# A gated mix of a state-space convolution and a linear attention on one core: the order of all steps, the engines of the evictions and the PSUM rings made anew

## The chip, the cores and the metric

The kernel runs on one core of one Trainium2 chip. The metric is the device time of one execution in microseconds (us); the times given are medians of several runs. A profile is taken of one execution. The core's engines are TensorE (PE; PEld is its weight load), VectorE (DVE), ScalarE (ACT), GpSimd (POOL) and SyncE (SP). SP only issues transfers and waits; the transfers themselves run on 16 DMA engines.

## The reference, cut to what matters

```python
# x, u: [1, 2048, 512] bf16
def _A_ref(u, ...):                       # a long convolution for each of 512 channels
    P = jnp.exp(logdA[:, :, None] * l)    # 512 channels x 128 states x 2048 steps
    K = jnp.einsum("dn,dnl,dn->dl", Cc, P, dB).real
    y = irfft(rfft(pad(u)) * rfft(pad(K)))[..., :L]
    return y + u * Dskip

def _B_ref(x, wqkv, w_phi, wo):           # 32 heads of 16
    q, k, v = split(x @ wqkv)
    phi_q = concat(softmax(q @ w_phi), softmax(-(q @ w_phi)))   # phi_k likewise
    kv = einsum("bhsf,bhsd->bhfd", phi_k, v);  z = phi_k.sum over s
    o = (phi_q @ kv) / (phi_q . z + 1e-6)
    return o @ wo

x = A_u
g = sigmoid((x * gate_w).sum(-1))
return g * _A_ref(x, ...) + (1 - g) * _B_ref(x, ...)
```

## The kernel before

The program is not written in the order in which it runs. Functions such as `prepare`, `attention_keys`, `plan_queries` and `plan_conv` add 1058 steps ("nodes") to a `Plan`, each with a name, an engine or a choice of two, the steps it depends on, and the buffers of named rings that it takes and gives back. `Plan.run` then calls the steps one after the other in the order that the string `ORDER` gives (two digits a step). Two more strings settle the choices: `SIDES` has a digit for each step that may run on either of two engines (nearly all of them copy a PSUM tile to SBUF: evictions), and `RINGS` has one for each PSUM tile that may come from either of two rings of two buffers, `ps`, and `p0` or `pf`. Each engine runs its own instructions strictly in the order in which they were recorded; what waits for another engine or a transfer holds all that stands behind it on that engine. For SP these are the issues of transfers: a transfer that waits for its data holds the transfers behind it.

```python
order = [64 * code[a] + code[b] for a, b in zip(self.ORDER[0::2], self.ORDER[1::2])]
...
n.at = n.eng if isinstance(n.eng, str) else n.eng[int(next(sides, 0))]
...
for i in order:
    n = self.nodes[i]
    ...
    n.fn()
```

In time the program has these stretches. (1) Loads, tables of sines, folding of w_phi into the weights (tiles wT, wps, WW, Wqp), transposes of x (xps to xT). (2) The keys of the attention in 16 blocks (pk, Ek, Zk, vp, vb, vr, kvp) with the first half of the Fourier transform of u beside them (psA to XAu, psB to xst, written to DRAM as XUd). (3) The second half of that transform with the polar tables of the convolution (Ctab, Dtab). (4) For 16 units of 32 channels: the kernel K of the convolution is made by a matmul of generated factors (cs, E, R, A to kps to KD), transformed (psA to XA, psB to XK), multiplied by u's transform, which is read back from DRAM (XUX; the product is t, lines L1231 and L1234), and transformed back (psz to Zr, written to DRAM as Zd and read back turned as ZT, then psy, then xT at L1367 or L1370); the queries of the attention run beside it (pq, Eq, apm, ax, ops, oT). (5) The last units, and the output's transfers (out_dram, L992 and L1384).

The channels are treated in four groups Q0 to Q3 of 128. Q0 to Q2 go through the transforms in one piece each; Q3 goes in three: 64 channels (units 12 and 13), 32 (unit 14) and 32 (unit 15, which skips the way over DRAM: tiles Z, L1373). In the profile the transfers of the first of these pieces are Zd_0_122, those of the second Zd_64_123. A product t needs a load XUX; there are three buffers for these loads. The string `FOURS` marks the units whose sum of two halves of A is left to TensorE (step A3, L1109, is then empty).

Of the kernel before, what the change touches and what calls it, by code (L numbers as in the profile page):

```python
# [70 lines left out]
class Plan:  # L71

    DIGITS = "0123456789abcdefghijklmnopqrstuvwxyzABCDEFGHIJKLMNOPQRSTUVWXYZ-_"
    ORDER = ("190H0I0405060B0C0D0d0e0f0y0z0A0s0t0u000K0L1d0J0M0S0U0V0N0_0P0Q2R11122x0O100W0T13142S0X0Y162T2U0708090g0h0i0j0k0l2y010203"
             "0m0n0o0a0b0c2V2X0Z15171a1H1b2v0R0-2Y2Z2W2L1c1n1o0p0q0r1w2M2-2_181y302J2K1e1f1p1z1A1I1J2w2B1x1E2D35312E1g1Y2C0v0w0x0E0F0G"
             "2F321N1B2G2H1C2I33361P372P1O2N341F382Q393b1q1r1s2O4C2z3c4J4K4L4M3d4Y4Z4-3a3e4N4O4_3f4Q3h3g1D4U3j4P1R4R4V4W4S5350573k4T3i"
             "511S544X52555b5c5d5e3l1G581Q3n595i5f5m3m5g3o1T5n5h5j565a3p3r3s5o1U3q3R5k3S5q5r5s5x1L4D5t3w4E3y5u3x3t3u3v5l5p5B5y5F1V5v5H"
             "3D1M5C3z2A5w5G3F5z5A5D3G4F5E5I5U5V5W3T3A3B3C3E5X5J5M5N5K5L5O4G5Q5Y5R5Z3K3M5S3U5_1Z635P5T3N5-1h1i1j1k1l1m6067691W643V6162"
             "65683H3I3J666m3W3L6o3O3P3Q3X3Z3-6a6n6p3Y6b6c1K6q3_6d6r6s414043421X441-27201_4546474828492129224a23246e2d2b252a4b4g4c2e2c"
             "2f2h1t1u1v266f2j2g4i4d4e4f2i4h4j4k4l4m4n2o2l2q2p6i2k2s4o4p4q4r4s4t2r6j4u4w4v4x2m2t2n6g6k6t4y4z4A6x6u2u8n6y6v4B8r6z8k8o8m"  # L80
             "8q6h6l6w6A6B8l6G8w4H8x8p8t4I6F8s8u6I6K8y6H8z6L8v8A8C9e9f9g8Q6M7d8D8I8E6N6J8R8B7f9b9c9d7g8F6O7h7j6P8S7i8G6Q8H8J8W8Z7Ma_b0"
             "b17k8K7e6R6S8T6C6D6E7O8-7Q6T8_8L7N7R8M8X6U6V6W937l8O8U8N8V7mae7S8P8Yaf7n7o94907p9192agan7Taoa4ap7q7P6X6Y6Z6_70716-7r7s7t"
             "a8a995a572ak73ah7u7v7w96aaa6ab9774at98aial7y7z7A7599a776aj9a7x77acau78am797aaqar9n9o7C9v7Uadasav9w7V9paw7B9xaKaLaBaC7D7W"
             "9q9raHaD9y7X7YaIaQaE9z9D9E7E7F7Zc5c6bXb_9L9Mc0aM7b9k9l9maFaxay9h9i9j9F7-7_80aGazaA7GbYc1aJ7HaR9A9B9C818283858687aNaOaP7I"
             "7cb-aYaZa-7JaSc784c3aT9Ncb88bZc8899s9t9uc29GaU9H9O8aaVc98b8dc49P9I9J9Kcc8fceaW8gcfaX7Kb5b6b78e8ccacdb8ckb97Lcgch8h8ibg8j"
             "cBclcibabhcCdYdZbocjcmbpcncDcHbicscvd-cIeLbb9Q9R9S9T9U9Vctcubjcyb2b3b4d_e0bq9W9X9YbccScTcU9Ze1e2eMbwbdbebfcwbke3co9-bxe4"
             "cPcQcRe5cqczblbmbncxe6e7e8cpbycreUdOeVcVcWcXcAcE9_cFcGa0eNa1dRcJe9eaebdSdTeRdWbrcKbscLcNeOePeSecbzcMcOc_bAdPdQedeeefeWd0"
             "dUeQbtbubvd1a2d7a3egd8bBbCbDeTdVcYcZc-d2e-d9dad3dfdneXbEbFbGdbe_bKeYbLdgdheZdodXfAf0d4d5d6dcdddefBdpbMdidqf1djehdrfCeibN"
             "fDf2bHbIbJf4g1f3eCeDeEdkdldmdsdtduf5bOf6fGg2fEf7fHfefFg7fIezeAeBfJffdBg4f8fgfKbPg3f9g5g8g6fLfadvdwdxbQfhdCdydzdAfbfcfddE"
             "fMdFfiejfNdGg9fjfkfldHekeFeGeHgaeleIeJeKgbepfmfnfoemgcfOfpfqfrfPeneofQbRbSbTeqerdDdIdJdKgdgegfgggifsghgjfRfSfTfUbUbVbWgk"  # L90
             "eseteuevfVfWfXfYfZf-glgmgngodLdMdNftfxfyfzgpfufvfwewexeygqgrf_g0gsgtgugvgwgx")
    SIDES = ("111110110010111010001100101000101000111000001011110000000000111110110001001110000010001000000000000000000000000000000000"
             "00000000000000000100000000000000000000000001011110101")
    RINGS = ("100100101110111011000000000000000000000000100000000000000000111101000000001010101111100111010001001100101011001111100110"
             "11000")
# [1535 lines left out]
```

## Time and profile before

| | |
|---|---|
| median of 3 runs | 263.15 us (263.0 to 264.77) |
| the profiled execution | 265.59 us, its span 263.8 us |
| busy, share of the span | DVE 88%, ACT 84%, PE 75%, PEld 51%, POOL 4% |
| mean granted TensorE clock | 0.92 |
| transfers | 36.19 MB, 137 GB/s in the mean |

The span runs from the first instruction to the last; 1.79 us of the execution lie around it. A share of busy time is a mean over the stretches above, which have different limits, so the prediction reads the busy time stretch by stretch. An engine's instructions overlap at their ends: two evictions of 128x1024 that take 1.02 us each stand in 1.94 us.

### The profile page before, as it was taken

What the parts mean: (1) busy time and instruction counts of PE and PEld (TensorE: products, weight loads), DVE (VectorE), ACT (ScalarE), POOL (GpSimd) and SP (SyncE); (2) the same over time, 40 slices, a digit from 0 to 9 for tenths busy, and PEclk for the clock granted to TensorE, in tenths of its full rate; (3) what the DMA queues carried; (4) which work ended last, traced back from release to release, by engine and by line L of the source; (5) the groups of instructions that cost most, each with busy time, mean ns of one, the idle gap of its engine ahead of it and who ended that gap; (6) DMA issues with size and microseconds to landing.
All of it is one profiled execution on the core that took longest, in us unless ns stands there. A gap on an engine that the chain in (4) does not pass through costs nothing.

```text
span 263.8 us, 10077 instructions
## 1 busy us (share of the span) xinstructions
PE 199.0 (75%) x4492; PEld 135.1 (51%) x4512; DVE 231.0 (88%) x314; ACT 221.2 (84%) x305; POOL 11.4 (4%) x22
## 2 busy tenths in 40 slices
PE   0576799999948569888498666799977698898650
PEld 0475566755735333445357354475864376774540
DVE  6799799898799998999999998999999989974440
ACT  7968998888899999999999999999999887665000
POOL 4650000000000000000000000000000000000000
PEclk9999999999995797999858988999999799999875
DMA  7799000362731676505250567366957788859875
GB/s 192 134 193 221 2 4 0 112 161 46 218 72 41 183 220 192 169 6 151 53 162 5 159 158 185 75 166 166 226 153 182 179 177 206 190 191 158 195 92 93
DMA packets 67259, 36.19 MB, mean 137 GB/s; under 512 B 46352, under 2 KB 62864, under 8 KB 66832
## 3 DMA queue, kind: packets, MB, share of 16 engines
q1 hardware_dynamic: 66160, 35.42, 55.2%
q8 instruction: 35, 0.57, 0.9%
q10 hardware_dynamic: 1056, 0.13, 0.3%
q14 instruction: 8, 0.07, 0.1%
HBM read 22.17 MB, written 13.37 MB: 135 GB/s over the span
## 4 chain that ended last, share of the span: by engine, by line
ACT 31%; PE 30%; DVE 22%; issue 7%; DMA 6%; POOL 1%; SPq 1%; ACTq 0%; DVEq 0%; POOLq 0%
ACT cs L68 6%; PE pk L705 5%; DMA XUX<-XUd 5%; PE vp L753 4%; ACT E L68 3%; PE psz L1263 3%; ACT Eq L68 3%; ACT XK L145 3%; ACT XA L145 2%; ACT Zr L145 2%; ACT xst L145 2%; PE kvp L770 2%; ACT L65 2%; PE psA L587 2%; PE psA L186 2%
## 5 line engine op out<-in xcount | busy, mean ns | idle before, releaser
L1098 DVE TENSOR_TENSOR A<-Ctab,Dtab 128x2048 bf16<-128x2048 bf16 x32 | 38.8, 1221 | 1.5 <-PE kps L179 1.5
L68 ACT ACTIVATE cs<-args 128x1024 bf16<-128x1024 f32 x32 | 30.8, 1060 | 0.5 <-PE args L1020 0.5
L179 PE MATMUL kps<-R,A 128*32 128x64 bf16 x1536 | 18.3, 205 | 6.9 <-issue 2.0
L179 PEld LDWEIGHTS <-A 128*32 128x32 bf16 x1536 | 16.2, 118 | 11.6 <-issue 5.9
L1116 DVE TENSOR_TENSOR R<-E,cs 128x2048 bf16<-128x2048 bf16 x16 | 19.5, 1221 | 0.6 <-ACT E L68 0.5
L1120 DVE TENSOR_TENSOR R<-E,cs 128x2048 bf16<-128x2048 bf16 x16 | 19.5, 1221 | 0.0
L68 ACT ACTIVATE Ek<-pk 128x512 bf16<-128x512 f32 x32 | 16.7, 603 | 2.5 <-PE pk L705 2.5
L1231 DVE TENSOR_TENSOR t<-XUX,XK 128x2048 bf16<-128x2048 bf16 x14 | 17.0, 1222 | 1.5 <-ACT XK L145 1.5
L145 ACT CAST XA<-psA 128x1024 bf16<-128x1024 f32 x15 | 15.2, 1040 | 3.3 <-PE psA L186 3.3
L145 ACT CAST Zr<-psz 128x1024 bf16<-128x1024 f32 x15 | 15.5, 1035 | 2.9 <-ACT cs L68 0.9
L1263 PE MATMUL psz<-t,TI 128*128 128x512 bf16 x53 | 16.0, 412 | 2.2 <-DVE xT L1370 0.6
L753 PE MATMUL vp<-WW,xT 128*128 128x512 bf16 x58 | 16.3, 406 | 1.0 <-issue 0.8
L68 ACT ACTIVATE E<-args 128x1024 bf16<-128x1024 f32 x16 | 16.8, 1059 | 0.2 <-PE args L1042 0.2
L839 PE MATMUL pq<-xT,Wqp 128*128 128x512 bf16 x64 | 16.5, 395 | 0.6 <-ACT Eq L68 0.6
L68 ACT ACTIVATE Eq<-pq 128x512 bf16<-128x512 f32 (+1 forms) x28 | 16.6, 698 | 0.1
L145 ACT CAST XK<-psB 128x1024 bf16<-128x1024 f32 x15 | 15.3, 1024 | 1.6 <-PE psB L192 1.5
L612 PE MATMUL psB<-XAu,TB 64*128 64x128 bf16 x256 | 11.3, 248 | 5.8 <-ACT xst L145 3.9
L705 PE MATMUL pk<-WW,xT 128*128 128x512 bf16 x58 | 14.7, 380 | 0.4 <-issue 0.2
L186 PE MATMUL psA<-W,KD 128*64 128x128 bf16 x256 | 11.2, 237 | 4.7 <-ACT cs L68 2.7
L612 PEld LDWEIGHTS <-TB 64*128 64x128 bf16 x256 | 9.4, 109 | 9.0 <-issue 8.9
L192 PE MATMUL psB<-XA,TB 128*128 128x128 bf16 (+2 forms) x192 | 10.2, 201 | 4.9 <-DVE XA L147 1.6
L186 PEld LDWEIGHTS <-KD 128*64 128x64 bf16 x256 | 9.2, 119 | 8.1 <-issue 5.7
(210 smaller groups left out, 503.5 us busy)
## 6 DMA issues: line engine op xcount, KB each, us to landing
XUX<-XUd SPq DMA_DIRECT2D x32, 256.0 KB, 4.1
XUd<-xst SPq DMA_DIRECT2D x8, 512.0 KB, 3.0
ax<-apd SPq DMA_DIRECT2D x16, 256.0 KB, 4.1
Zd<-Zr SPq DMA_DIRECT2D x15, 256.0 KB, 3.0
ZT<-Zd SPq DMA_DIRECT2D x12, 256.0 KB, 5.4
UD<-in_A_u_dram SPq DMA_DIRECT2D x16, 128.0 KB, 4.3
XUd<-xst SPq DMA_DIRECT2D x8, 256.0 KB, 3.8
wqk<-in_B_wqkv_dram SPq DMA_DIRECT2D x1, 1024.0 KB, 6.5
```

The lines of the kernel that those rows point to most:

```text
L68: return self.nc.scalar.activation(**kw)
L145: self.nc.scalar.copy(out=o, in_=i)
L179: nc.tensor.matmul(kps[32 * dj:32 * dj + 32, g4, e, :], lhsT=A[:, d // 4, 32 * ka:32 * ka + 32, d % 4], rhs=R[:, kr, d, :], start=(i == 0) ...
L186: nc.tensor.matmul(ps[64 * ri:64 * ri + 64], lhsT=lhsT, rhs=fc.W1[:, ri].rearrange("p r d -> p (r d)"), start=True, stop=True, tile_positi ...
L612: nc.tensor.matmul(box.ps[:, c2, sl, :], lhsT=fc.TB[rows, b0:b0 + 2].rearrange("p a b -> p (a b)"), rhs=X.t[rows, k, r0 + sl].rearrange("p ...
L705: nc.tensor.matmul(box.ps[:], lhsT=xT[:, st, kt, :], rhs=g.WW[:, kt, :], start=(kt == 0), stop=(kt == 3))
L753: nc.tensor.matmul(box.ps[:], lhsT=xT[:, st, kt, :], rhs=g.WW[:, 4 + kt, :], start=(kt == 0), stop=(kt == 3))
L1098: nc.vector.tensor_tensor(out=c.A[:, :, 64 * k:64 * k + 64, :].rearrange("p q (x b) l -> p x b q l", b=8), in0=cf.unsqueeze(2).to_broadcas ...
L1116: nc.vector.tensor_tensor(out=c.R[:, :, :, 32:64], in0=t.E[:, 1].unsqueeze(1).to_broadcast([128, 2, 32, 32]), in1=t.cs[:], op=ALU.mult)
L1120: nc.vector.tensor_tensor(out=c.R[:, :, :, 0:32], in0=t.E[:, 0].unsqueeze(1).to_broadcast([128, 2, 32, 32]), in1=t.cs[:, ::-1, :, ::-1], o ...
L1231: nc.vector.tensor_tensor(out=box.t, in0=Ls[r0 // ns].X[:], in1=box.XK[:].unsqueeze(1).to_broadcast([128, 2, 1024]), op=ALU.mult)
L1263: nc.tensor.matmul(box.ps[:, hb, :], lhsT=fc.TIp[:, k].rearrange("p h a t -> p (h a t)"), rhs=box.t[:, k, 512 * hb:512 * hb + 512], start= ...
```

## The change

`ORDER`, `SIDES` and `RINGS` are replaced. No step is added or removed, the rings have as many buffers as before, and `FOURS`, which marks eight units, reads the same.

```diff
 class Plan:
-    ORDER = ("190H0I0405060B0C0D0d0e0f0y0z0A0s0t0u000K0L1d0J0M0S0U0V0N0_0P0Q2R11122x0O100W0T13142S...
+    ORDER = ("0405060B0C0D0H0d0e0f0y0z0A190s0t0u0708090I0J0M000L11120g0h0i0j0k0l0K0102030_2R0S0T10...
...
-    SIDES = ("111110110010111010001100101000101000111000001011110000000000111110110001001110000010001...
+    SIDES = ("101110000101100010001000101110100001101100001011100000000000000000100010010100101001000...
...
-    RINGS = ("100100101110111011000000000000000000000000100000000000000000111101000000001010101111100...
+    RINGS = ("000111101111001111000000000000000000000000100000000000000010001110100000101010101101010...
...
     FOURS = ("0111100101011000")
```

Of the steps with a choice of engine, 24 go from DVE to ACT (8 vb, 3 xT of the transposes, 3 oT, 2 XK, 2 xst, and one each of XAu, KD, wT, wps, Z and the Ctab copy of psy), 17 from ACT to DVE (4 of L978, 3 oT, 2 XAu, 2 xst, 2 vb, 2 xT of the transposes, one UDp, one xT of bps), and one from POOL to DVE (Wphi, L469). Three places of the order follow.

SP, the last stretch. The rows are transfers: XUX is a load of u's transform for unit 12 and up, Zd and ZT the way of a piece over DRAM and back, out_dram the output. Before:

```order
L1289 DMA ZT<-Zd_0_121 32x4096 x4
L1279 DMA Zd_0_122<-Zr 128x1024 x2
L1185 DMA XUX<-XUd 128x1024 x4
L1289 DMA ZT<-Zd_0_122 32x32x64 x4
L1384 DMA out_dram<-xT 32x12x256 x2
L1384 DMA out_dram<-xT 32x12x128 x2
L1279 DMA Zd_64_123<-Zr 128x1024
L1384 DMA out_dram<-xT 32x12x256 x2
L992 DMA out_dram<-xT 32x4x384 x2
L1289 DMA ZT<-Zd_64_123 32x32x32 x4
L1384 DMA out_dram<-xT 32x12x128 x2
L1384 DMA out_dram<-xT 512x1x64 x4
```

Four more stand behind these rows: two of L992 and two of 512x1x64. The same stretch after the change:

```order
L1185 DMA XUX<-XUd 128x1024 x2
L1289 DMA ZT<-Zd_0_121 32x4096 x4
L1279 DMA Zd_0_122<-Zr 128x1024 x2
L1185 DMA XUX<-XUd 128x1024 x2
L1289 DMA ZT<-Zd_0_122 32x32x64 x4
L1384 DMA out_dram<-xT 32x12x128 x4
L1279 DMA Zd_64_123<-Zr 128x1024
L1384 DMA out_dram<-xT 32x12x256 x4
L1289 DMA ZT<-Zd_64_123 32x32x32 x4
L1384 DMA out_dram<-xT 512x1x64 x2
L992 DMA out_dram<-xT 32x4x384 x2
L1384 DMA out_dram<-xT 512x1x64 x2
```

One of the two last loads has moved ahead of the four ZT of Q2. Both output transfers of Q2 (32x12x128), of which one stood behind ZT of the second piece, now stand ahead of Zd_64_123; the rest of Q1's output (32x12x256) stands between that Zd and its ZT, and both pairs of L992 are behind it.

ACT, from the last table load on (the load that goes from the sine set back to the exponential set). psz to Zr evicts an inverse transform, psA to XA and psB to XK a forward one, kps to KD a kernel, ops to oT the attention. Before:

```order
L65 ACT_TABLE_LOAD
L68 ACTIVATE E<-args 128x1024
L145 CAST KD<-kps 128x1024
L145 CAST Zr<-psz 128x2x8x64 x2
L145 CAST oT_4895<-ops 128x1024
L145 CAST XA<-psA 128x32x32 x2
L68 ACTIVATE E<-args 128x1024
L145 CAST XK<-psB 128x1024
L145 CAST KD<-kps 128x512
L145 CAST XK<-psB 128x1024
L145 CAST XA<-psA 128x1024
L145 CAST Zr<-psz 128x1024
```

After:

```order
L65 ACT_TABLE_LOAD
L145 CAST Zr<-psz 128x2x8x64
L145 CAST KD<-kps 128x1024
L145 CAST Zr<-psz 128x2x8x64
L68 ACTIVATE E<-args 128x1024
L145 CAST XA<-psA 128x32x32 x2
L68 ACTIVATE E<-args 128x1024
L145 CAST XK<-psB 128x1024 x2
L145 CAST KD<-kps 128x512
L145 CAST Ctab_74<-psy 128x4x128
L145 CAST Zr<-psz 128x1024 x2
L145 CAST XA<-psA 128x1024
```

The oT eviction has moved ahead of the load, and XA of the next unit behind the two Zr of the 64-channel piece; the first E has moved behind the two Zr of Q2.

DVE in the same stretch, from the last product t of Q2 on. A and R are the factors of units 14 and 15, E is the product with G. Before:

```order
L1231 TENSOR_TENSOR t<-XUX,XK 128x2048
L1370 TENSOR_TENSOR xT<-psy,gT 128x8x128
L1050 TENSOR_TENSOR E<-E,Gtab 128x1024
L1098 TENSOR_TENSOR A<-Ctab_75,Dtab 128x64x8x4
L1116 TENSOR_TENSOR R<-E,cs 128x64x32
L1098 TENSOR_TENSOR A<-Ctab_75,Dtab 128x64x8x4
L1120 TENSOR_TENSOR R<-E,cs 128x64x32
L1109 TENSOR_TENSOR A<-A 128x8x256
L1116 TENSOR_TENSOR R<-E,cs 128x64x32
L1098 TENSOR_TENSOR A<-Ctab_75,Dtab 128x64x8x4
L1231 TENSOR_TENSOR t<-XUX,XK 128x2048 x2
L1367 TENSOR_TENSOR xT<-psy,gT 128x4x128
```

After:

```order
L1231 TENSOR_TENSOR t<-XUX,XK 128x2048
L1370 TENSOR_TENSOR xT<-psy,gT 128x8x128
L1098 TENSOR_TENSOR A<-Ctab_75,Dtab 128x64x8x4 x2
L1050 TENSOR_TENSOR E<-E,Gtab 128x1024
L1116 TENSOR_TENSOR R<-E,cs 128x64x32
L1109 TENSOR_TENSOR A<-A 128x8x256
L1120 TENSOR_TENSOR R<-E,cs 128x64x32
L1231 TENSOR_TENSOR t<-XUX,XK 128x2048
L1367 TENSOR_TENSOR xT<-psy,gT 128x4x128
L1231 TENSOR_TENSOR t<-XUX,XK 128x2048
L1116 TENSOR_TENSOR R<-E,cs 128x64x32
L1050 TENSOR_TENSOR E<-E,Gtab 128x1024
```

The first R and the first A of unit 15 have moved behind the two products t of the 64-channel piece; the product at L1367 stands between these two.

More of the change, by code (lines that the diff above doesn't have):

```diff
@@ L73 @@
     DIGITS = "0123456789abcdefghijklmnopqrstuvwxyzABCDEFGHIJKLMNOPQRSTUVWXYZ-_"
[L74 to L95, printed above, removed]
+    ORDER = ("0405060B0C0D0H0d0e0f0y0z0A190s0t0u0708090I0J0M000L11120g0h0i0j0k0l0K0102030_2R0S0T100W0U0Y2x0V130P0Q2S0N2T0X2y2U142V0O0R"
+             "160Z0m0n0o0a0b0c0p0q0r152X2J2Z170-0v0w0x182-1a1b1y1c0E0F0G1n1d2W2K1o2_1e1w1z2Y1H1A2D1x301f2E2L1p1I1E1J1S312M2B2C1g1C3235"
+             "361B37381P2F2G2H1q1r1s2I33341F2N2O2v2P2Q2z4C393b3c4J4L3a3d3f4Y4K4M1t1u1v1R3g4-4Z3e4_4N3h4Q3j504R3i4O3l513k4P4S4U3n4V4W1Y"
+             "1N3o3m5357584T4X1D5b1G5254593R5c553S5d5e5i5m5j5n3p3r3s5f5g561O5a5q5r5s5h5t5o5x5y1L5k1T4D2w4E3q5u5v5B5l4F5p3w5C3y3x3z3t3u"
+             "3v5F5H3D5w5D3F5z1Z5A5E3E5G5U5W5I1U5J5V3A3B3C3G3T5X5M5Q5K3K5R5L4G5S5N3M5_1V1M5Y5O5Z5-63645P5T1Q67606169653N2A683L62663U1W"
+             "6a6m6n6o6p1h1i1j3V3W6b1K6c3X6q3Y3Z6r1k1l1m6d3_3-416e6s401X1-3H3I3J4243451_272021442829223O3P3Q47482a4649232d2e4b2b2f244a"
+             "2c2o4c252g4g4i2h4h2i4j6f2p2j4d4e4f4k4l4m2q2k2l264n4p4o2m4q2s6t2r4u4v6g2n4r4s4t6i2t4w6h6u4x2u6j8m6k6x8q6v8k8o6y6l6z4y4z4A"
+             "6w6A6B8l8p8n8r8s4B8w8x6G8t8y6I8u4H8C4I6J8v8D8z8A8Z8E6K6L8I6M6H6F6C6D6E8B6N8F8-8J7d6O8_7e6P9b9c9d8Q8R6Q7M8G7f7N6R7g7h6S9k"
+             "9l9m6T8H8K7i7O7j8S8L8W937P8T7k8M8N8Xan7Q6U6V6W8Uao7l8V8O7m9e9f9g948P6X6Y6Z7R7n7o8Y907p7S6_7071aeaf91ag92a47q6-7r7s7tap95"
+             "7Taha8a972a5ai96akaaat73a675ab77979878ajal999aaua7ac7u7v7w7x74am7976aqaras9n7U9o9vadav9p9waK7C7VaEaw9q7WaL7aaB7b9xaQaM7X"
+             "7Y9raRaC7y7z7A7D9y9z9h9i9j7Z9D9Eb5b6b7c5c6aFbX9F7c7Eb_7B9L9Mc0axayaDaH7G9NbYc19A9B9C7IaG9GaI9HazaAaJ7F7H7J7-7_80b-818283"
+             "84898bc38c8aaNbZaO9s9t9uaPaSc2aTc7858687c4888d9O8f8gc88ececfaYaZa-7K7Lcbc9cc9Pck8haU8ia_b0b18jcBaVca9I9J9KaWaXcdcgclchcC"
+             "b8bgb99Q9R9Sba9T9U9VcsctcicHcjbhbobpdYcDbicId-dZeUcmd_bbbjcncybce0bweV9Ze1cvcwbxb2b3b4cVcWcXe2bkbdbebf9W9X9Ycxco9-cue3e4"
+             "czblbmbnbqcpcqdOe5creLcAcEeMbycFa0e6e7e8a1dSa2dTa3brcGcJbsbzcK9_eWeNeOcLcPcQcRe9eaebbAeceRcMcNdPedeeefegcOc_dUbtbubvd0eh"
+             "bBbCbDcScTcUePeSeid1eQd7d8dQdfe-dVeTbEbFbGd2d9daeXdge_cYcZc-bHbIbJd3d4d5d6dbdndRdcdddeeYbKdhdWdoezeAeBdieZeCeDeEdXbLdpdj"
+             "dkdldmbMf0f1dqdrfAfBfDfEf2f4bNg1f5fCf3fGbOfFg2f6f7fefHdBf8bPfffgdsdtdufIfJg7g3eIeJeKbQf9dvdwdxfafKdydzdAfhfidCg4dEdFfLfb"
+             "fcfdfMg8fjfkfldGeFeGeHdHfmfnfog5fNg6fOejekfPfpfqfreldDg9gadLdMdNfQgbgcepdIdJdKemgdgeeneogffRfSfTfUbUbVbWeqbRbSbTggfsfVfW"
+             "fXgighgjftgkglgmgngoeresfYfZf-fxfyfzewexeyfufvfwgqf_gpgreteuevg0gvgwgxgsgtgu")
@@ L96 @@
+    SIDES = ("101110000101100010001000101110100001101100001011100000000000000000100010010100101001000010000000000000000000000000000000"
+             "00000000000000000000000110110000000000000000011000001")
+    RINGS = ("000111101111001111000000000000000000000000100000000000000010001110100000101010101101010110011001010100110010011001111001"
+             "11110")
     WARM = ("000000000000000000000000000000000000000000000000000000000000000000000000000000000000000000000000000000000000000000000000"
```

## The prediction

> **What bounds the kernel now.** I read the page's busy times first, then cut the span where the limits change and asked for the busy time of each engine in each stretch, then followed SP, ACT and DVE through the end in the timeline. The cuts are: the first evictions of the keys (30), the table load into the polar stretch (its end, 75.3), the end of the load out of it (105), the last table load (about 216), the last A of unit 15 (234.4), the stretch in which the last piece runs (249).
>
> ```profile
> PE 199.0 (75%) x4492; PEld 135.1 (51%) x4512; DVE 231.0 (88%) x314; ACT 221.2 (84%) x305; POOL 11.4 (4%) x22
> ```
>
> Columns below: start and end, length, busy time (instructions) of PE, PEld, DVE, ACT and POOL, granted clock, share of the DMA engines, GB/s.
>
> ```profile
> 0.00:30.00 30.00, 15.13 (x159) 13.39 (x160) 25.66 (x62) 24.42 (x31) 11.44 (x22) 1.00 0.80 163
> 30.00:75.30 45.30, 43.46 (x763) 27.87 (x770) 39.65 (x52) 39.86 (x75) 0.00 (x0) 1.00 0.32 87
> 75.30:105.00 29.70, 20.05 (x312) 11.37 (x315) 28.78 (x54) 29.50 (x34) 0.00 (x0) 0.77 0.48 141
> 105.00:216.00 111.00, 87.95 (x2276) 58.41 (x2279) 107.66 (x115) 107.34 (x141) 0.00 (x0) 0.92 0.53 139
> 216.00:234.40 18.40, 16.03 (x410) 12.56 (x411) 17.87 (x18) 13.46 (x15) 0.00 (x0) 1.00 0.73 179
> 234.40:249.00 14.60, 11.18 (x308) 7.21 (x309) 8.11 (x12) 6.07 (x10) 0.00 (x0) 1.00 0.98 205
> 249.00:263.80 14.80, 5.21 (x294) 4.29 (x286) 3.27 (x5) 0.58 (x1) 0.00 (x0) 0.62 0.64 99
> ```
>
> No single engine binds. In 30 to 75.3 PE does (43.46 of 45.3), and both evicting engines have 5 to 6 us to spare. In 75.3 to 105 ACT is full. In 105 to 216 DVE and ACT are both at 97%, so an eviction moved there gains nothing: what one engine saves the other pays. From 216 DVE is full and ACT has 4.9 us idle; from 234.4 no engine is full, the DMA engines are (0.98), and after 249 nothing is. The last 29 us hold what an order can still win. SP shows why:
>
> ```profile
> 231.93 1.74 SPq L1279 DMA_DIRECT2D Zd<-Zr  x2
> 233.77 1.83 SPq L1185 DMA_DIRECT2D XUX<-XUd  x4
> 235.92 5.20 SPq L1289 DMA_DIRECT2D ZT<-Zd  x4
> 241.54 3.31 SPq L1384 DMA_DIRECT2D out_dram<-xT  x4
> 244.95 0.59 SPq L1279 DMA_DIRECT2D Zd<-Zr  x1
> 245.58 1.19 SPq L1384 DMA_DIRECT2D out_dram<-xT  x2
> 246.88 2.01 SPq L992 DMA_DIRECT2D out_dram<-xT  x2
> 249.00 2.98 SPq L1289 DMA_DIRECT2D ZT<-Zd  x4
> 252.02 6.80 SPq L1384 DMA_DIRECT2D out_dram<-xT  x6
> 258.87 1.11 SPq L992 DMA_DIRECT2D out_dram<-xT  x2
> 260.07 1.25 SPq L1384 DMA_DIRECT2D out_dram<-xT  x2
> ```
>
> From 235.92 to 261.32 SP issues 27 transfers almost without a pause, 0.94 us each, and the span ends 2.5 us after the last. DVE's last product, on which only the last pairs depend, had ended at 256.88 (below). So the end of the kernel is the start of that run of issues plus what they take. The run starts with ZT of the 64-channel piece, which waits for the landing of the second Zd (issued by 233.67, 2.25 us earlier), and that waits for the Zr at 232.27:
>
> ```profile
> 212.67 1.94 ACT L145 CAST XK<-psB 128x1024 bf16<-128x1024 f32 x2
> 214.63 1.28 ACT L65 ACT_TABLE_LOAD   x1
> 220.42 1.02 ACT L145 CAST oT<-ops 128x1024 bf16<-128x1024 f32 x1
> 229.88 1.01 ACT L145 CAST XA<-psA 128x1024 bf16<-128x1024 f32 x1 [2.29 <-PE psA L186]
> 232.27 1.03 ACT L145 CAST Zr<-psz 128x1024 bf16<-128x1024 f32 x1
> ```
> ```profile
> 214.87 1.22 DVE L1109 TENSOR_TENSOR A<-A 128x2048 bf16<-128x2048 bf16 x1
> 225.14 1.23 DVE L1116 TENSOR_TENSOR R<-E,cs 128x2048 bf16<-128x2048 bf16 x1 [0.51 <-ACT E L68]
> 227.42 2.36 DVE L1231 TENSOR_TENSOR t<-XUX,XK 128x2048 bf16<-128x2048 bf16 x2
> 238.81 0.69 DVE L1234 TENSOR_TENSOR t<-XUX,XK 128x1024 bf16<-128x1024 bf16 x1 [1.37 <-DMA XUX<-XUd]
> 241.44 0.69 DVE L1234 TENSOR_TENSOR t<-XUX,XK 128x1024 bf16<-128x1024 bf16 x1 [1.94 <-DMA XUX<-XUd]
> 242.05 1.22 DVE L1370 TENSOR_TENSOR xT<-psy,gT 128x1024 bf16<-128x1024 f32 x1
> 256.19 0.69 DVE L1370 TENSOR_TENSOR xT<-psy,gT 128x512 bf16<-128x512 f32 x1 [0.52 <-PE psy L1345]
> ```
>
> **The change, part by part.** The seven units that leave sums to TensorE are not in the diff: the string that marks units reads the same and the eight sums of L1109 stand in both programs, so this is worth nothing.
>
> ```profile
> L1109 DVE TENSOR_TENSOR A<-A 128x2048 bf16<-128x2048 bf16 x8 | 9.8, 1222 | 0.0
> L147 DVE CAST vb<-vp 128x512 bf16<-128x512 f32 x10 | 6.7, 684 | 0.0
> L145 ACT CAST vb<-vp 128x512 bf16<-128x512 f32 x6 | 3.5, 587 | 0.0
> L147 DVE CAST XAu<-psA 128x1024 bf16<-128x1024 f32 x8 | 9.6, 1221 | 3.1 <-PE psA L587 3.1
> L145 ACT CAST XAu<-psA 128x1024 bf16<-128x1024 f32 x8 | 7.9, 1018 | 0.6 <-PE psA L587 0.6
> L147 DVE COPY xT<-xps 128x1024 bf16<-128x1024 bf16 x4 | 2.8, 688 | 0.0
> L145 ACT COPY xT<-xps 128x1024 bf16<-128x1024 bf16 x4 | 4.1, 1017 | 2.5 <-PE xps L500 2.5
> L978 ACT ACTIVATE xT<-bps,gT 128x384 bf16<-128x384 f32 x4 | 2.2, 585 | 0.0
> L469 POOL TENSOR_TENSOR Wphi<-wc,mask 128x512 bf16<-128x512 bf16 x1 | 1.6, 1629 | 4.7 <-DMA wc<-in_B_w_phi_dram 4.7
> ```
>
> *Engines.* Net of exchanges, ACT takes 6 vb (6 x 0.587 = 3.5), one wps, one wT and one xT (1.0 each, by the rows of that width), and at the end two half XK, a Z, a Ctab copy and a small KD (about 2.7); it gives four of L978 (2.3), a UDp, an XAu (1.0 each) and a small xT (0.4). Sum +4.5. DVE gives 6 vb (4.1), a wps (1.2), a wT and an xT (0.7 each) and the five of the end (3.2); it takes an XAu (1.2), UDp and small xT (0.4 each), four of L978, which before never ran on DVE (128x512 takes 0.684, 128x256 about 0.42; I take 0.56, 2.2 in all), and Wphi (no DVE row of it: between 0.4, a copy's price, and POOL's 1.63; I take 0.7, the price of DVE's products of that size). Sum -4.9. The total hardly falls; it is shifted from DVE to ACT. Behind the last table load ACT's gains and losses cancel, and the oT of the row at 220.42 moves ahead of it, so 5.5 us more stand ahead of that load, or 4.4 once the 0.1 us by which queued instructions overlap (1.02 against 0.92, at 212.67) is taken off each: 3.0 in stretches one and two, 0.9 to 105, 0.5 to the load. On DVE 3.4 us less stand ahead of the sum at 214.87.
>
> *To 75.3.* DVE's work ahead of the first XAu falls by 2.4 us (wps, wT, xT and a fill of the polar tables that now comes later, against UDp and Wphi), where it had 4.3 us idle of 30. ACT's rises by 1.9, with 5.6 us idle there. The input loads are issued in the same order, so they give nothing. I take 1.0 us, between 0 and 2.4. From then on PE binds, so ACT's 6 vb go into its 5.4 us of idle; one group of psA now stands behind the keys (about 0.45 us of PE less ahead of them). Sum -1.5. If the idle of ACT cannot be filled, it is +3.0.
>
> *75.3 to 105.* ACT is full, with one psA eviction more: +0.9, between 0 (DVE's idle of 0.9 is no help) and +1.5.
>
> *105 to 216.* ACT +0.5, DVE +0.6 (in the order the products of neighbouring units change places across the cut). Each had about 3.5 us idle of 111. Whether new waits arise the trace of before can't show: all idle gone is -3.0, twice the idle +3.5. I take the idle as it was: +0.5.
>
> *216 to the second Zd.* From the load's start to the end of that Zr are 18.7 us. ACT's 13 evictions and exponentials of 128x1024 in it stand 0.92 us apart where they queue (1.94 less 1.02 at 212.67); with the load and two small ones that is 14.3, and 4.4 idle. Without oT and with XA of the next unit behind the two Zr it is 12.4 of work. On DVE the R and A of unit 15 (2 x 1.14, the distance at 227.42) leave the way of the two t, a product of 0.6 comes between, and the wait of that R for its E (0.51 before 225.14) is no longer ahead: t ends 2.2 us sooner. Then one XA eviction less before the Zr: 0.9. Sum -3.1, and I take -3.0. Bounds: 0 if t waits for XK as long as before, -6.3 if ACT decides and has no idle left (18.7 less 12.4). What is late next is the XUX of unit 15's first product, still issued behind that Zd.
>
> *The 27 issues.* They are the same in number. One XUX pair goes ahead of ZT of Q2, whence its product (241.44) can follow the other at once, 2.0 us sooner; but the place it frees, between Zd and ZT, was hidden behind Zd's landing. Both Q2 output pairs now stand ahead of Zd of the second piece; they wait for the product at L1370 (242.05), and behind them on SP are that Zd, Q1's output, ZT, and everything to the end. By the rows: ZT of the first piece ends 7.5 us after the second Zd; the product, now 2.0 sooner, 7.5 us after it. So SP is held for next to nothing. Bounds: -2.4 (the 0.5 MB of the moved XUX at 205 GB/s, taken out of the full stretch) and +3.3 (the product no sooner, 2.0, and the four issues at the 1.13 of the six at 252.02 and not at 0.83, 1.2). I take 0.
>
> Sum: -1.5 + 0.9 + 0.5 - 3.0 + 0 = **-3.1 us**. The profiled execution took 265.59 (span 263.8 and 1.79 around it), which gives 262.5; the median of the runs lies 2.44 under it, which gives 260.0.
>
> On the end the Trainium skill speaks against the change. DMA: Bandwidth & Descriptors, section Issuing engines are not separate DMA queues, says that starting a transfer costs sequencer time that is usually small beside the transfer itself. Here the rows show 25.4 us of issues in the last 29, and a DMA share of 0.98 beside them to 249 but 0.64 after, so the trace agrees with the page for the first half at most. By the page the order of issues is worth nothing and the sum would be that of the third rival below.
>
> **Rivals.**
> - *ACT binds (slower).* The place is ACT's queue ahead of the last table load, the price the 4.4 us that it gets, and the point from which it decides is its idle ahead of that load: 0 to 216 less 201.1 busy, 14.9 us. If these waits are PE's and the loads', they stay, the load comes 4.4 later, and DVE waits for E behind it; the 3.0 behind the load are then lost to full DMA engines. 263.15 + 4.4 = 267.6. For it: 75 to 216 has no ACT idle to speak of. Against: 11 of the 14.9 lie before 75.3.
> - *Better packing.* The idle of 105 to 216 goes too (-3.0): 257.0. Nothing but the room speaks for it.
> - *Transfers set the end.* DMA share 0.98 from 234.4 to 249: if those bytes bind, an earlier Zd only finds the engines busy with the moved XUX and the 3.0 are given back: 263.0. Against: in 216 to 234.4 the share is 0.73, so there is room to start sooner.
> - *It does not do what it says.* True of the sums, without effect.
>
> **How the numbers follow.** Forecast 0.46, around 260.0, two thirds of it under 260.5; ACT binds 0.17; better packing 0.12; transfers set the end, or losses elsewhere that cancel the gain, 0.25. About 1% (2.6 us) is what a measurement of this kernel can tell from no change. Faster by more: 0.31 + 0.12 = 0.43; within: 0.15 + 0.25 = 0.40; slower: 0.17. The range of 256.0 to 267.0 holds all cases up to most of the slow one and of the well packed one; the forecast's own is 257.5 to 262.0.
>
> **What would show it.** ACT busy near 225.7 and DVE near 226.1. Right: the table load into the polar stretch ends 1 to 2 us before 75.3; the last load starts near 214.5; the second Zd of the 64-channel piece is issued 15 to 16.5 us after it (19.0 before); from the ZT behind it still about 25 us of issues. Wrong: that load starts at 217 or later (ACT binds), more than 5 us idle on DVE in the long stretch, or SP held ahead of the Q2 output for over 2 us.

## The result, and the profile after

The change makes the kernel faster by 1%: 260.0 us against 263.58 in the first comparison (ratio 0.9898, 95% interval 0.9862 to 0.9934), 260.4 against 262.89 in a second one (0.9878, 0.9852 to 0.9904). A ratio is taken over the single runs, without those over 1.5% above the fastest of their kernel, and is therefore not the quotient of the two medians. By the ratios the gain is 2.7 and 3.2 us, by the medians 3.6 and 2.5; the forecast was a gain of 3.1 and a time of 260.0.

The two profiled executions differ by more, 265.59 against 259.96. The one before was an unusually long one: 84 further runs of that kernel lay between 260.97 and 264.9. Most of what it lost it lost between 105 and 216, as two experiments with the very same steps there show below.

The page after, busy times, and the stretches (start and end, length, busy time of PE, PEld, DVE, ACT and POOL, granted clock, DMA share, GB/s):

```profile
PE 197.2 (76%) x4512; PEld 132.2 (51%) x4512; DVE 227.3 (88%) x308; ACT 224.4 (87%) x312; POOL 11.2 (4%) x21
```
```profile
30.00:75.30 45.30, 43.90 (x771) 27.60 (x770) 38.57 (x53) 42.13 (x82) 0.00 (x0) 1.00 0.31 86
75.30:105.00 29.70, 20.53 (x310) 11.52 (x310) 28.71 (x53) 29.66 (x33) 0.00 (x0) 0.71 0.54 161
105.00:216.00 111.00, 86.97 (x2356) 57.64 (x2356) 108.81 (x117) 107.48 (x142) 0.00 (x0) 0.97 0.52 138
216.00:234.40 18.40, 16.93 (x392) 12.76 (x391) 16.83 (x17) 13.58 (x17) 0.00 (x0) 1.00 0.83 226
234.40:249.00 14.60, 11.26 (x451) 7.77 (x449) 8.77 (x14) 4.70 (x10) 0.00 (x0) 1.00 0.79 142
249.00:258.20 9.20, 1.39 (x75) 0.84 (x75) 1.12 (x2) 0.00 (x0) 0.00 (x0) 0.53 0.60 103
```

The load of ACT and DVE moved the way that was forecast, by less: ACT +3.2 us and DVE -3.7, where +4.5 and -4.9 were expected. Of the DMA engines, 216 to 234.4 now uses more (0.83, before 0.73) and 234.4 to 249 less (0.79, before 0.98): transfers moved into the room that was there.

SP's issues at the end (start, length, transfer, count), and the products, the sum and the loads on which they hang, on DVE and ACT:

```profile
218.48 2.26 SPq L1185 DMA_DIRECT2D XUX<-XUd  x2
222.21 2.50 SPq L1289 DMA_DIRECT2D ZT<-Zd  x4
227.44 1.85 SPq L1279 DMA_DIRECT2D Zd<-Zr  x2
229.41 1.09 SPq L1185 DMA_DIRECT2D XUX<-XUd  x2
232.23 3.27 SPq L1289 DMA_DIRECT2D ZT<-Zd  x4
236.95 3.00 SPq L1384 DMA_DIRECT2D out_dram<-xT  x4
240.06 0.43 SPq L1279 DMA_DIRECT2D Zd<-Zr  x1
240.53 3.18 SPq L1384 DMA_DIRECT2D out_dram<-xT  x4
243.83 3.54 SPq L1289 DMA_DIRECT2D ZT<-Zd  x4
...
254.43 1.27 SPq L1384 DMA_DIRECT2D out_dram<-xT  x2
```
```profile
223.00 1.23 DVE L1231 TENSOR_TENSOR t<-XUX,XK 128x2048 bf16<-128x2048 bf16 x1
...
224.74 1.22 DVE L1231 TENSOR_TENSOR t<-XUX,XK 128x2048 bf16<-128x2048 bf16 x1
...
233.36 1.23 DVE L1109 TENSOR_TENSOR A<-A 128x2048 bf16<-128x2048 bf16 x1
234.51 1.28 DVE L1234 TENSOR_TENSOR t<-XUX,XK 128x1024 bf16<-128x1024 bf16 x2
235.71 1.22 DVE L1370 TENSOR_TENSOR xT<-psy,gT 128x1024 bf16<-128x1024 f32 x1
```
```profile
72.53 1.28 ACT L65 ACT_TABLE_LOAD   x1
...
213.85 1.28 ACT L65 ACT_TABLE_LOAD   x1
```

The sum of unit 15 (L1109) ends at 234.59, where it ended before (234.38), by this row of the profile before:

```profile
233.16 1.22 DVE L1109 TENSOR_TENSOR A<-A 128x2048 bf16<-128x2048 bf16 x1
```

What is new is what follows it. Before, the two products at L1234 started at 238.81 and 241.44 and waited for XUX; now both follow the sum at once, because one XUX was issued at 218.48 and the other at 229.41 (before, both stood behind Zd, at 233.77 to 235.60). So the product at L1370 comes at 235.71 and not at 242.05, and the last issue ends at 255.70 and not at 261.32.

### The profile page after: what moved, and what is told of

Read it like the earlier page. It is cut to its first block, busy times and chain, and to the rows that moved or that the text cites. A ratio compares the mean times of both kernels' runs of the same rounds, so it can differ in the third digit from the quotient of the medians.

```text
span 258.2 us, 10095 instructions
## 1 busy us (share of the span) xinstructions
PE 197.2 (76%) x4512; PEld 132.2 (51%) x4512; DVE 227.3 (88%) x308; ACT 224.4 (87%) x312; POOL 11.2 (4%) x21
## 4 chain that ended last, share of the span: by engine, by line
ACT 43%; PE 35%; issue 7%; SPq 7%; DVE 4%; DMA 2%; ACTq 0%
ACT cs L68 9%; PE pk L705 6%; ACT Eq L68 5%; PE vp L753 4%; SPq L1497 4%; ACT XA L145 4%; ACT E L68 4%; PE psz L1263 3%; ACT L65 3%; ACT XK L145 3%; ACT Zr L145 3%; ACT xst L145 3%; PE psy L820 3%; PE kps L179 2%; ACT trg L68 2%
## 5 line engine op out<-in xcount | busy, mean ns | idle before, releaser
L179 PE MATMUL kps<-R,A 128*32 128x64 bf16 x1536 | 17.3, 199 | 7.9 <-DVE R L1120 1.9
L179 PEld LDWEIGHTS <-A 128*32 128x32 bf16 x1536 | 15.4, 116 | 11.9 <-DVE R L1120 4.0
L1263 PE MATMUL psz<-t,TI 128*128 128x512 bf16 x60 | 15.7, 387 | 3.4 <-ACT cs L68 1.5
L145 ACT CAST XK<-psB 128x1024 bf16<-128x1024 f32 (+1 forms) x17 | 16.8, 1016 | 0.4 <-PE psB L192 0.4
L753 PE MATMUL vp<-WW,xT 128*128 128x512 bf16 x64 | 17.0, 398 | 0.0
L705 PE MATMUL pk<-WW,xT 128*128 128x512 bf16 x64 | 15.2, 380 | 0.0
L612 PEld LDWEIGHTS <-TB 64*128 64x128 bf16 x256 | 10.0, 114 | 9.5 <-issue 9.0
L762 DVE TENSOR_TENSOR vr<-vb,vr 128x1024 bf16<-128x1024 bf16 x16 | 10.6, 688 | 3.0 <-ACT vr L68 2.7
L147 DVE CAST XAu<-psA 128x1024 bf16<-128x1024 f32 x9 | 10.6, 1218 | 2.7 <-PE psA L587 2.7
```

The source lines that it names most:

```text
L145: self.nc.scalar.copy(out=o, in_=i)
L179: nc.tensor.matmul(kps[32 * dj:32 * dj + 32, g4, e, :], lhsT=A[:, d // 4, 32 * ka:32 * ka + 32, d % 4], rhs=R[:, kr, d, :], start=(i == 0) ...
L612: nc.tensor.matmul(box.ps[:, c2, sl, :], lhsT=fc.TB[rows, b0:b0 + 2].rearrange("p a b -> p (a b)"), rhs=X.t[rows, k, r0 + sl].rearrange("p ...
L705: nc.tensor.matmul(box.ps[:], lhsT=xT[:, st, kt, :], rhs=g.WW[:, kt, :], start=(kt == 0), stop=(kt == 3))
L753: nc.tensor.matmul(box.ps[:], lhsT=xT[:, st, kt, :], rhs=g.WW[:, 4 + kt, :], start=(kt == 0), stop=(kt == 3))
L1263: nc.tensor.matmul(box.ps[:, hb, :], lhsT=fc.TIp[:, k].rearrange("p h a t -> p (h a t)"), rhs=box.t[:, k, 512 * hb:512 * hb + 512], start= ...
```

## The experiments

The first kernels are merges of the two programs: the steps of one stretch are arranged (order, engines, rings) as before or as after the change. The others are the kernel after with single steps moved. Lines behind the tables are 19 lower in their rows, since the tables fill fewer lines. The ratio always is to the kernel before. The marks are those of each kernel's profiled execution, in us: "Zd" is the end of the issue of the second Zd of the 64-channel piece, "end" that of SP's last issue. Each column is counted from the one before it. The marks are those of one execution, and the ratio is that of all: the profiles of x1, x0 and v2 lay 1.7, 1.2 and 2.1 us under the medians of their kernels, those of x2 and y4 2.2 and 3.1 over.

| kernel | ratio (95% interval) | load into polar stretch ends | to the end of the load out of it | to the last load | to Zd | to the end |
|---|---|---|---|---|---|---|
| before | 1 | 75.30 | 29.65 | 109.67 | 19.04 | 27.65 |
| x1_head | 1.0034 (1.0013 to 1.0056) | 74.31 | 30.84 | 107.54 | 18.80 | 26.81 |
| x2_middle | 1.0078 (1.0048 to 1.0107) | 75.30 | 31.14 | 110.10 | 18.14 | 28.20 |
| x3_tail | 0.9925 (0.9891 to 0.9959) | 75.12 | 30.05 | 107.34 | 17.92 | 25.75 |
| z1_middle_and_tail | 0.9936 (0.9903 to 0.9969) | 75.76 | 30.28 | 109.85 | 15.31 | 26.54 |
| after | 0.9898 (0.9862 to 0.9934) | 73.81 | 30.29 | 109.75 | 15.44 | 26.41 |
| x0_after, the same again | 0.9878 (0.9852 to 0.9904) | 75.07 | 30.29 | 108.80 | 14.97 | 25.83 |
| w3_products_late | 1.0004 (0.9976 to 1.0032) | 74.44 | 30.29 | 110.33 | 17.58 | 26.76 |
| y1_xux_back | 0.9973 (0.9944 to 1.0001) | 74.66 | 31.26 | 110.03 | 15.06 | 27.81 |
| y2_outs_back | 0.9932 (0.9905 to 0.9959) | 73.75 | 30.29 | 109.46 | 14.98 | 27.83 |
| y3_q1_early | 0.9882 (0.9847 to 0.9918) | 73.62 | 30.30 | 111.13 | 14.89 | 25.85 |
| w1_sp_order | 0.9893 (0.9855 to 0.9930) | 74.62 | 31.22 | 109.90 | 15.16 | 26.25 |
| v2_one_issuer | 0.9895 (0.9852 to 0.9939) | 73.51 | 30.28 | 109.32 | 15.73 | 25.74 |
| y4_act_issues | 1.0071 (1.0044 to 1.0098) | 73.93 | 30.29 | 110.05 | 15.71 | 33.49 |

### One stretch alone, and the whole

```diff
 x1: steps up to the table load into the polar stretch
-    as before
+    as after
```


> Before, with the steps up to the table load into the polar stretch arranged as after the change (order, engines, rings); everything behind as before. Theory that the gain adds up by stretch (head -1.5, middle +0.7, end -3 to -5 us): 1.5 us faster than before, ratio about 0.994, that load ends at 73.8 instead of 75.3, and all later marks lie 1.5 earlier. Rival, that the long stretch gives the head's gain back: ratio 1.000, the load at 73.8 but the last table load starts within 0.3 us of where it did. Rival, that the whole difference of the profiles is chance of the one profiled execution: the load itself stays at 75.3.

```diff
 x2: steps from there to the last table load
-    as before
+    as after
```


> Before, with only the steps from the table load into the polar stretch up to the last table load arranged as after the change. Theory of sums by stretch: 0.1 to 0.7 us slower than before (the first half of the stretch +0.6, the second +0.1), ratio 1.000 to 1.003, the last load starting 0 to 0.7 later. Rival, that the new middle only fits the new head (its ACT has one more psA eviction): over 1.5 us slower. Rival, better packing in the middle: the last load 1 us or more earlier.

```diff
 x3: steps behind the last table load
-    as before
+    as after
```


> Before, with only the steps behind the last table load arranged as after the change. Theory of sums by stretch: the second Zd of the 64-channel piece is issued 15 to 16 us after the start of that load (19.0 before) and the kernel is 3 to 4.5 us faster, ratio 0.983 to 0.989, 24 to 25 us from the ZT behind that Zd to the end of issues. Rival, transfers set the end: the Zd earlier, but 28 us of issues behind it and a ratio of 0.997 or more. Rival, the end only gains because the middle has already done part of its work: under 1 us faster.

> The changed kernel itself beside the three parts on one chip. If the parts add up, its difference from before is the sum of the three (about -4 us by the medians known, ratio 0.985 to 0.99); if they depend on one another the sum is off by over 1 us.

Measured, in us of 262.89: head +0.9, middle +2.05, end -2.0; sum +1.0. The whole change is -3.2. The parts do not add up, by 4 us: the theory of sums by stretch falls.

The head alone does bring the load into the polar stretch forward (74.31), and the next stretch gives it back (30.84 us, 29.65 and 30.05 with the old head). ACT there, in the view of waits of x1 (who, waited for what: us, times, longest); before has no such wait:

```profile
ACT trg L68 <- DVE Dtab L360: 0.9, 1, 0.9
```

By these marks the head alone is worth nothing. Why it is 0.9 us slower in the time they do not show, since this execution lay 1.7 us under the median, and it stays open.

The end alone meets waits that neither program has there. DVE behind the last load of x3, which starts at 212.51 (in brackets the idle time ahead of an instruction):

```profile
217.48 2.36 DVE L1079 TENSOR_TENSOR A<-Ctab,Dtab 128x2048 bf16<-128x2048 bf16 x2 [1.04 <-PE kps L160]
220.65 0.69 DVE L1031 TENSOR_TENSOR E<-E,Gtab 128x1024 bf16<-128x1024 bf16 x1 [0.81 <-ACT E L68]
```

The new end counts on work that the new middle has done ahead of the load (the oT that the prediction saw leave the stretch behind it, among others). Without it DVE waits 1.04 us for PE and 0.81 for ACT, and Zd comes 17.92 after the load and not 15.

x1 and x3 also settle the odd profile of before. Their steps from 105 to the last load are those of before, and they took 107.54 and 107.34 us for them, where the profiled execution of before took 109.67. So 2.2 of its 2.44 us above the median lie there and belong to no step of the program; x3's own execution lay 0.2 under its median. The idle time there was not the usual one either. From the end of the load out of the polar stretch to the last load, before (first row) and in x3, DVE and ACT are busy for the same time, but before has 3.3 and 3.6 us idle beside it and x3 1.1 and 1.3:

```profile
104.95:214.63 109.68, 86.63 (x2235) 57.50 (x2239) 106.34 (x114) 106.10 (x142) 0.00 (x0) 0.92 0.53 138
105.16:212.51 107.35, 85.61 (x2240) 57.02 (x2239) 106.21 (x114) 106.04 (x142) 0.00 (x0) 0.94 0.55 142
```

```diff
 z1: steps behind the table load into the polar stretch
-    as before
+    as after
```


> Before up to the table load into the polar stretch, and everything behind it arranged as after the change. Theory that middle and end belong together (the new middle pays about 2 us for steps that the new end then no longer has) and that the head is worth nothing or less: 3.2 to 4.1 us faster than before, ratio 0.984 to 0.988, that is as fast as the whole change or faster. Rival, the head is worth its 1 to 1.5 us when the new middle follows it: 1.7 to 2.2 us faster than before, ratio 0.991 to 0.994. Rival, sums by stretch: the middle's +2.05 and the end's -2.0 as measured alone give no change, ratio 1.000.

-1.7 us, the range of the rival by which the head is worth 1 to 1.5 us when the new middle follows (0.9936 against 0.9878 with it is 1.5 us; the two intervals just touch). The middle, which alone cost 2.05 us, costs 0.3 us when the new end follows (z1 against x3). The rival of x2 had the size right and named the head; it is the end that takes up most of this cost. The head, +0.9 alone and -1.5 in front of both, fits them too.

### The products on DVE put later

```diff
 DVE, behind the R of unit 14, after the change
+R of unit 15 (L1116), its E (L1050)
 t of the 64-channel piece (L1231)
-xT (L1367)
 t of the 64-channel piece (L1231)
+xT (L1367)
-R of unit 15 (L1116), its E (L1050)
 ACT
+XA of unit 14
 Zr x2
-XA of unit 14
```


> After, with the two products of the 64-channel piece put later on DVE (the factor R of unit 15 with its E and ahead of them, as R stood before the change) and XA of unit 14 ahead of the two Zr on ACT, as before the change. The prediction's step for the end (the Zr sooner by 3 us, so the ZT and the run of issues behind it sooner) expects that Zd is issued 1.5 to 2 us later and the end moves with it: ratio 0.994 to 0.997. Rival: DVE is full to the products of unit 14 at 235 in either order, and those, which before waited for XUX, set the end; then Zd comes 1.5 to 2 us later and the end less than 0.5 us: ratio 0.986 to 0.990.

The whole gain is gone (1.0004; 3.3 us against 0.9878, where the prediction's step expected 1.5 to 2.4). The rival, by which a late Zd moves the end by less than 0.5, falls. Zd is issued 17.58 us behind the load, 2.3 later than in the other kernels with the new steps, and the end lies another 0.7 later behind it. Behind that Zd, SP and DVE of the run show:

```profile
231.38 1.25 SPq L1260 DMA_DIRECT2D Zd<-Zr  x2
232.75 0.85 SPq L1166 DMA_DIRECT2D XUX<-XUd  x2
```
```profile
235.37 1.22 DVE L1090 TENSOR_TENSOR A<-A 128x2048 bf16<-128x2048 bf16 x1
238.12 1.29 DVE L1215 TENSOR_TENSOR t<-XUX,XK 128x1024 bf16<-128x1024 bf16 x2 [1.52 <-DMA XUX<-XUd]
```

A late Zr holds Zd on SP, and Zd holds the XUX that stands behind it in SP's queue. The next products, which have nothing to do with that piece, then wait 1.52 us for it again. So w3 delays Zd and this load together, and does not show what the late Zd costs by itself.

### SP's issues one at a time

```diff
 SP, after the change
-XUX (the second of the last two loads) x2
 ZT of Q2 x4
 Zd of the 64-channel piece x2
 XUX x2
+XUX (the second of the last two loads) x2
 ZT of the 64-channel piece x4
```


> After, with one pair of issues alone put back where it was: the last XUX behind the other one, between Zd of the 64-channel piece and its ZT. Theory that the place of SP's issues counts: the second product L1234 waits for it again, the output pairs of Q2 are held behind that product, and the end comes 1.5 to 3 us later than after the change, ratio 0.993 to 0.999. Theory of the prediction (the place it frees is hidden behind Zd's landing, the product's 2.0 us are held back elsewhere): under 0.5 us, ratio 0.988 to 0.990. Rival, transfers set the end: no change, ratio 0.988.

```profile
236.78 0.69 DVE L1215 TENSOR_TENSOR t<-XUX,XK 128x1024 bf16<-128x1024 bf16 x1 [1.54 <-DMA XUX<-XUd]
238.23 0.69 DVE L1215 TENSOR_TENSOR t<-XUX,XK 128x1024 bf16<-128x1024 bf16 x1 [0.76 <-DMA XUX<-XUd]
```

Ratio 0.9973, 2.5 us over 0.9878: without the move of this one pair most of the gain is gone. Both products wait, not the second alone; presumably the two loads, issued one behind the other, share the DMA engines. Zd comes when it came (15.06), and from it to the end are 27.81 us as before the change.

The pair changes a second thing, the issues of the ZT behind it:

```profile
233.44 5.33 SPq L1270 DMA_DIRECT2D ZT<-Zd  x4
```

They took 3.27 and 3.61 us in the two profiles after the change and 5.20 before. y1 does not tell how much of the 2.5 us is the late products and how much these issues.

```diff
 SP: ZT of Q2 x4
+out_dram of Q1 x2
 Zd of the 64-channel piece x2, XUX x2, ZT x4
+out_dram of Q1 x2
 out_dram of Q2 x4, Zd of the second piece
-out_dram of Q1 x4
 ZT of the second piece x4
```


> After, with the two pairs of Q1's output (ready since the product at about 225) issued earlier: one behind the ZT of Q2, where SP is idle until the first Zd, the other behind ZT of the 64-channel piece, where SP waits 1.1 to 1.5 us for the product of Q2. Both leave the way between Zd and ZT of the second piece. Theory that issues set the end: ZT of the second piece starts at about 242.4 instead of 243 to 243.8, SP has 3 us less behind it, 1.5 to 2.5 us faster than after, ratio 0.978 to 0.982. Rival, transfers set the end, or the earlier transfer slows the last loads: within 0.5 us of after, ratio 0.986 to 0.990.

No change (0.9882), as the rival had it. The wait that SP had behind ZT is filled, and the product ahead waits instead. And at the very end SP waits for a transfer of ACT, which it does not after the change (view of waits of SP):

```profile
235.99 1.29 DVE L1215 TENSOR_TENSOR t<-XUX,XK 128x1024 bf16<-128x1024 bf16 x2 [1.59 <-DMA XUX<-XUd]
```
```profile
SPq L1365 <- DMA out_dram<-xT: 1.3, 1, 1.3
```

```diff
 SP: Zd of the 64-channel piece x2, XUX x2
+out_dram of Q1 x2
 ZT of the 64-channel piece x4
+out_dram of Q1 x2
 out_dram of Q2 x2
-out_dram of Q2 x2
 Zd of the second piece
-out_dram of Q1 x4
+out_dram of Q2 x2
 ZT of the second piece x4
```


> After, with SP's last stretch ordered so that it neither waits for the product of Q2 nor holds Zd of the second piece: one pair of Q1's output behind the last XUX, the other behind ZT of the 64-channel piece, one pair of Q2, then that Zd as soon as its Zr is there, the other pair of Q2 behind it. Theory that SP's issues set the end: ZT of the second piece starts at about 240.5 instead of 243 to 243.8 and the end comes 1.5 to 2.4 us sooner than after, ratio 0.978 to 0.982. Rival, the chain of products and landings (XUX, product, Zr, Zd, ZT, last product) sets the end and SP's issues only fill it: that ZT 1 to 2 us sooner but less than 0.7 us in the time, ratio 0.985 to 0.990.

No change either (0.9893, in the range of the rival), and here no product waits. The rows from ZT on, and SP's wait at the very end:

```profile
233.76 4.26 SPq L1270 DMA_DIRECT2D ZT<-Zd  x4
238.06 3.48 SPq L1365 DMA_DIRECT2D out_dram<-xT  x4
241.65 0.58 SPq L1260 DMA_DIRECT2D Zd<-Zr  x1
...
254.80 2.35 SPq L1365 DMA_DIRECT2D out_dram<-xT  x2
```
```profile
SPq L1365 <- DMA out_dram<-xT: 1.2, 1, 1.2
```

Part of what SP no longer waits for it spends in issues: ZT takes 4.26 us (3.27 after the change). One pair fewer stands between the two ZT, and the second ZT starts no sooner (29.3 us behind the last load; 30.0 and 28.8 in the two profiles after the change). The last pair's 2.35 us (1.27 after the change) are not two longer issues: between them SP waits 1.2 us until a transfer of ACT on the same semaphore has landed, of the pair that ACT issues behind the very last product (y2, below, has how semaphores are shared). After the change SP's last issue starts at 255.05, and the transfer of ACT on its semaphore has landed at 254.75 (254.30 and 254.10 in the second profile): only 0.2 to 0.3 us could be gained there by issuing sooner. The theory that SP's issues set the end misses its 1.5 to 2.5 us here and with y3; but in both 1.2 to 1.3 us of what SP saved are lost at this wait, so they do not refute it, and transfers and the chain of products remain as rivals.

```diff
 SP: ZT of the 64-channel piece x4
+out_dram of Q1 x2
-out_dram of Q2 x4
+out_dram of Q2 x2
 Zd of the second piece
-out_dram of Q1 x4
+out_dram of Q1 x2
 ZT of the second piece x4
+out_dram of Q2 x2
```


> After, with the output pairs of Q1 and Q2 in the order of before: one pair of Q1 directly behind the ZT of the 64-channel piece (where after the change SP waits 1.1 to 1.5 us for the product of Q2), one pair of Q2, Zd of the second piece, the other pair of Q1, ZT of the second piece, and only then the other pair of Q2. Number and bytes are the same. Theory that issues set the end: the wait is filled, 1 us faster than after, ratio 0.983 to 0.985. Rival, transfers or the chain of products sets the end: within 0.5 us of after, 0.986 to 0.990. Rival, the change's place for these pairs was worth something: 0.992 or more.

0.9932, slower than after by 1.4 us against 0.9878 (by 0.9 against the first comparison), the third of the cases. But the pairs of Q1 and Q2 themselves show no harm. In its profile ZT of the second piece comes 1 to 2 us earlier after the last load than after the change (27.8 us; 28.8 and 30.0), and SP is then held later, by the view of waits and in the timeline:

```profile
SPq L973 <- DMA out_dram<-xT: 3.1, 1, 3.1
```
```profile
249.85 1.25 SPq L1365 DMA_DIRECT2D out_dram<-xT  x2
254.18 0.80 SPq L973 DMA_DIRECT2D out_dram<-xT  x2
```

The program hands its transfers out to eight semaphores in turn, SP's and ACT's together, and an issue waits for the last transfer on its semaphore, as the numbers of the semaphores in the traces show. The pair of L992 (here L973) had got the one of a pair that ACT issues only behind the very last product, at 251.88. The waits at the end of y3 and w1 are of this kind too.

```diff
 as y2, and
-SP: out_dram x2, L992 x2, out_dram x2, L992 x2, out_dram x2;  ACT: out_dram x2
+SP: L992 x4, out_dram x8
```


> After, with the output pairs of Q1 and Q2 in the order of before (one of Q1 fills the wait behind ZT of the 64-channel piece, the other of Q2 behind ZT of the second piece), the two pairs of L992 next, and the last two pairs both issued by SP: ACT issues nothing. With that order of Q1 and Q2 alone SP stood 3.1 us at a pair of L992 whose lane had been handed to a transfer that ACT issued only at the very end. Theory that this wait was the loss: no such wait, the issues end 39.5 to 40.5 us after the start of the last table load (40.8 and 41.9 after the change, 42.8 with that order alone) and the ratio is 0.983 to 0.986, faster than after. Rival, the output order of the change is the better one by itself: 0.990 to 0.994 as with that order alone. Rival, transfers set the end: as after, 0.987 to 0.989.

```profile
248.34 6.24 SPq L1365 DMA_DIRECT2D out_dram<-xT  x8
```

The wait is gone, but the eight issues behind the pairs of L992 end 41.5 us after the start of the last load, not 39.5 to 40.5: two of them were ACT's before. That is as after the change (40.8 and 41.9) and less than with y2 (42.8), and so is the time, 0.9895, between the ranges of the two rivals; its interval also holds y2's ratio, so what the wait cost is shown by the profiles alone. No order of the outputs that was tried beats the change.

```diff
-SP: out_dram (512x1x64, first pair), L992 x4
+ACT: the same three pairs
```


> After, with three output pairs of the last stretch (the two of L992 and the first of the 64-channel piece) issued by ACT, which has nothing else to do there, instead of SP. The bytes and their number are the same; SP has 4.6 us of issues less behind the last ZT. Theory that issues set the end: SP's last pair then waits for the last product only, the end comes 2 to 2.5 us sooner than after, ratio 0.979 to 0.981. Rival, transfers set the end: each issue takes longer for it, ratio 0.986 to 0.990. Rival, ACT's issues hold its own last pair: the end moves to ACT and 1 us or less is gained.

Slower than before (1.0071), 5 us over after, where 2 faster were expected. The same semaphores are the reason that its profile shows (it is of an execution of 268.15, above the median of 265.1, so only what SP waits for is read from it, which the order of the program fixes):

```profile
SPq L1365 <- DMA out_dram<-xT: 8.8, 2, 8.1
```
```profile
243.54 10.80 SPq L1365 DMA_DIRECT2D out_dram<-xT  x4
254.43 4.31 SPq L1270 DMA_DIRECT2D ZT<-Zd  x4
```

SP stands at Q1's output until a transfer of ACT has landed, and ZT of the second piece starts at 254.43 instead of 243.83. So this run does not tell issues from transfers: it tells that an issue moved to an idle engine can hold those that stay.

## Why the prediction was right, and where not

- **Total and subtraction.** 260.0 forecast; 260.0 and 260.4 measured. That the profile of before lay 2.44 above its median was taken off rightly: 2.2 of it were lost in steps that took 107.4 us in two other executions.
- **To 75.3: -1.5.** The load into the polar stretch ends at 74.17 in the mean of the ten profiles with the new head and at 75.37 in the four with the old one: -1.2. It is worth that only with the new middle; alone the head is 0.9 slower.
- **75.3 to 105: +0.9.** 30.5 us (mean of nine) against 29.85 (two): +0.65.
- **105 to 216: +0.5.** This term was mis-sized. The new middle takes 109.9 us to the load (mean of eleven), the old one 107.4 in x1 and x3: +2.4. "I take the idle as it was" is the step that failed: the 3.5 us of idle in the one profile were 2 us more than usual, so that the idle did not stay but rose, on DVE from 1.1 and 1.3 us (x3, x1) to 2.2 and 1.6 (the two profiles after the change). The work was undercounted as well: DVE has 1.2 us more of it ahead of the load, among it one sum of L1109, where the working had 0.6.
- **216 to the second Zd: -3.0.** Measured 15.2 us (mean of the eight kernels with the new steps and Zr not put late, 14.9 to 15.7) against 18.9 (before and x1): -3.7, of which some is that same work done ahead. The gain goes when Zd is late (w3), but the load behind it is late with it there; and with Zd in time and that load late (y1) most of it goes too. So an early Zd is not enough alone; a late Zd with the load in time was not run.
- **The 27 issues: 0.** Too little gain. From Zd to the end 26.1 us remain after the change (two profiles) of 27.2 before (before and x1): -1.1, inside the bounds of -2.4 and +3.3. From the first ZT on, the issues took 23.5 and 23.0 us, where the sign of being right was still about 25. The working saw that the product comes 2.0 us sooner and that the Q2 output, unit 14's Zd and its ZT, which stand behind one another on SP, need it; its bound "the product no sooner, 2.0" is near the 2.5 that y1 shows. What it put at nothing is the place of the XUX pair, "hidden behind Zd's landing": without that pair the ZT behind it takes 1.6 to 1.9 us less.
- **The outputs.** That part holds: they may stand in four orders with 0.9878 to 0.9895, as long as no shared semaphore holds SP for as long as in y2 and y4. v2, where SP issues everything and ACT nothing, agrees with the Trainium skill, DMA: Bandwidth & Descriptors, section Issuing engines are not separate DMA queues, by which the engine that starts transfers matters little, as all share the same DMA engines; y4, 5 us slower for the semaphores, does not. Of the order of issues the section says nothing; that it is worth nothing was the prediction's own step, and y1 refutes it.
- **Rivals.** ACT does not bind as that rival had it: the last load starts at 213.85 and not at 217 or later. Against x3's 212.51 it is 1.3 us later all the same, which may be a part of the rival's 4.4. The middle is not better packed, it got longer. That transfers set the end and give the whole gain back is not what came (260.0 and 260.4, not 263.0), and the share of the DMA engines between 234.4 and 249 fell from 0.98 to 0.79. Whether they limit what is left of the end stays open; y3 came out in the range that this rival had there.

The errors of the third term (about 2 too good) and of the last two (about 2 too bad) cancel, and that is luck. The time was right by its sum, the direction by the fourth term, and the size of the parts was not.

## What to carry to other kernels

Ask of a queue of transfers not how many issues it has but which load stands behind an issue that still waits for its data; putting one such load back cost 2.5 of the 3.2 us here. Stretches of an order belong together: measure a stretch alone and it can look like a loss (two of three here) that is a gain with its neighbour. Before forecasting from one profiled execution, ask where it lies among the runs, and do not size idle time by it if it is the longest.
